# GpSimd powers in place of VectorE reciprocals for the softmax row sums of a fused attention and MLP kernel

## Chip, cores and metric

One NeuronCore of a Trainium2 chip runs the whole kernel. The metric is the device time of one execution in microseconds (us), the median of three runs.

## What is computed

Block-causal attention (8 batches, 8 heads, 576 positions, head size 64, blocks of 64), and on its output, laid out as 4608 tokens of 512 channels, a two-layer MLP with a squared ReLU:

```python
scores = scale * np.matmul(q, k.transpose(0, 1, 3, 2))
scores = np.where(block_i >= block_j, scores, -1000000000.0)
scores = scores - np.max(scores, axis=-1, keepdims=True)
attn = np.exp(scores)
attn = attn / (np.sum(attn, axis=-1, keepdims=True) + 1e-09)
x = np.matmul(attn, v)            # then transposed to tokens x channels
r = np.maximum(x @ w_in, 0.0)
out = (r * r) @ w_out
```

The change touches the division by the row sums.

## The kernel before

**Passes and groups.** Attention goes in 40 passes, each for a pair of heads of one batch: passes 0 to 7 (the first 192 positions of batches 0 and 1), 8 to 11 (the other positions of batch 0) and 12 to 39. A pass works on one to three groups of blocks of 64 query rows; the two heads fill the 128 partitions. There are 8 groups in passes 0 to 7 and three in each of the 32 others, 104 in all. A group has two, three or four blocks, so its row sums are a tile of 128 partitions by 2, 3 or 4 (`sm`).

**The steps of a group** are closures made by `rows` (line 781) and `splits`, and named by a letter and the group (`R21_2` is step R of pass 21, group 2):

- A: TensorE computes the scores into a two-bank PSUM tile (`side`).
- B: VectorE takes each row's negated maximum (`nmx`).
- C: ScalarE takes the exponential into the f32 tile `p` (two buffers; four slots of `p_rows` in passes 0 to 7) and accumulates the row sum into `sm`.
- S (`summed`, line 822): GpSimd adds 1e-9 to `sm` and scales it by a power of two.
- R (`inverse`, lines 826 to 828): VectorE takes the reciprocal of `sm` into `rs`. This is the line that changes.
- Then `p` is multiplied by `rs`. In passes 0 to 7 step D (VectorE or GpSimd) makes three diagonal matrices of `rs`, with which TensorE transposes and scales at once. In passes 8 to 11 step D (ScalarE, VectorE) writes the scaled rows. From pass 12 on, step H (ScalarE or VectorE) writes an f16 high part and step L (VectorE) the f16 rest, into `p_rows`; one step per piece of a row, `H21_2_1` being piece 1 of group `21_2`.
- From pass 12 on the rows are turned by DMA transposes issued by SP (T); then TensorE multiplies by the values (G) and the result is read out (X).

The buffer of `p` is free for a later group's C when the group's last L (or D) is done.

**The MLP** runs between these steps. TensorE multiplies in `pair` and `single` PSUM tiles; ScalarE and VectorE rescale, square and split the hidden layer into f16 parts (`r`, `hidden`), and the residual `hidden<-r,hidden` (steps `rem`) is taken by GpSimd or VectorE. In the first 120 us the weights are loaded and split into f16 parts as well: `bits` on GpSimd, `join` and `low` on VectorE, `cast` on any of the three. The normalized tokens are split by steps `t` and `s`, some on GpSimd.

**The order** is written out by hand. `ORDER` (from line 104) lists every step, with a letter where an engine has to be chosen (A ScalarE, D VectorE, P GpSimd). `Plan.run` walks through it, and the wrapper `Queue` chains each engine's instructions, so that every engine works in the order of this list, whatever is ready. A step R stands at its own place in the list, often long after its S. In 49 of the 104 groups at least one other GpSimd step stands between the two; six of them have only other S steps between. Two of the places, cut to those steps that matter here (lines 123 to 124 and 174 to 177):

```
... cast0_14:P ... R11_2 D11_1:D max1_9:A sq0_1_0 D11_2:D ...
... R21_1 po2_1_10 l232_1 H21_1_1:A S21_2 t2_15:P H21_1_2:A H21_1_0:A p64_0 a114_0 t3_9:P R21_2 L21_1_2 ...
```

Of the kernel before, what the change touches and what calls it, by code (L numbers as in the profile page):

```python
# [8 lines left out]
F32 = mybir.dt.float32  # L9
# [6 lines left out]
ALU = mybir.AluOpType  # L16
# [3 lines left out]
P = 128  # L20
# [377 lines left out]
def attention_moe_kernel(ctx: ExitStack, tc: tile.TileContext, qk1, v1, qk, ks, vm, vt, w_in, w_out, out):  # L398
    nc = Lines(tc)
    NB = vm.shape[0]  # L400

    const = ctx.enter_context(tc.tile_pool(name="const", bufs=1))
# [10 lines left out]
    def bank_of(ring):  # L413

        turns_of[ring] += 1
        return homes[ring][(turns_of[ring] - 1) % len(homes[ring])]
# [8 lines left out]
    nc.vector.memset(zero, 0.0)  # L425
    ones_bf = const.tile([P, P], BF16, name="ones_bf")
    nc.vector.memset(ones_bf, 1.0)
    vd = const.tile([P, 2], BF16, name="vd")
    nc.gpsimd.memset(vd, 0.0)

# [100 lines left out]
    def spin(region, n):  # L531


        w = region.shape[-1]
        for _ in range(n):
            nc.tensor.matmul(
                region.rearrange("p (a b) -> p a b", b=D),
                ones_bf,
                ones_bf[:, None, 0:D].to_broadcast([P, w // D, D]),
                start=True,  # L540
                stop=True,
            )
# [217 lines left out]
    def scores(t, ps, group):  # L760


        lanes = ([], [])
        for j, off in group:
            c0 = 0
            while c0 <= j:
                c1 = min(j + 1, c0 + 8 - (off // D + c0) % 8)
                o = off + D * c0
                lanes[o >= 512 if t["quad"] else 0].append((j, c0, slice(o, off + D * c1)))
                c0 = c1  # L770
        order = [(z, x) for n in range(4) for z in range(2) for x in lanes[z][n : n + 1]]
        for z, (j, c0, o) in order:
            k = slice(D * c0, D * c0 + o.stop - o.start)
            keys = t["turned"] if z else t["kf"]
            q = t["turned"][:, S:] if z and j == NJ - 1 else t["qf"][:, D * j : D * j + D]
            for r in range(2):
                rs = slice(D * r, D * r + D)
                h = 1 - r if z else r
                nc.tensor.matmul(ps[D * h : D * h + D, o], q[rs], keys[rs, k], start=True, stop=True)

    def rows(t, group):

        u = t["u"]
        n = len(group)
        gu = f"{u}_{group[0][0]}"
        box = {}
        short = t["whole"] and not t["first"]
        at = {2: 0, 1: 2 * P, 0: 3 * P} if short else dict(group)

        def score():  # L790
            ps = box["ps"] = bank_of("s")
            if t["i"] == 0:
                spin(ps[:, 512:], SPIN)
            scores(t, ps, group)

        def largest():
            ps = box["ps"]
            nmx = box["nmx"] = small.tile([P, n], F32, tag="nmx", name=f"nmx_{gu}")
            for i, (j, off) in enumerate(group):
                w = D * (j + 1)  # L800
                nc.vector.tensor_reduce(nmx[:, i : i + 1], ps[:, off : off + w], axis=AX.X, op=ALU.max, negate=True)
            nc.vector.tensor_scalar(nmx, nmx, D**-0.5, None, op0=ALU.mult)

        def raised():
            if short:
                p32 = x_rows[:, t["i"] % SLOTS].rearrange("p b k -> p (b k)")
            else:
                p32 = p2.tile([P, 1024], F32, tag="p32", name=f"p32_{gu}")
            box["p32"] = p32
            sm = box["sm"] = small.tile([P, n], F32, tag="sm", name=f"sm_{gu}")  # L810
            for i, (j, off) in enumerate(group):
                w = D * (j + 1)
                nc.scalar.activation(
                    p32[:, at[j] : at[j] + w],
                    box["ps"][:, off : off + w],
                    AF.Exp,
                    bias=box["nmx"][:, i : i + 1],
                    scale=D**-0.5,
                    accum_out=sm[:, i : i + 1],
                )  # L820

        def summed():
            sm = box["sm"]
            nc.gpsimd.tensor_scalar(sm, sm, 1e-9, 2.0**-A_P, op0=ALU.add, op1=ALU.mult)

        def inverse():
            rs = box["rs"] = small.tile([P, n], F32, tag="rs", name=f"rs_{gu}")
            nc.vector.reciprocal(rs, box["sm"])

        def spread(q="DVE"):  # L830
            if short:
                (nc.vector if q == "DVE" else nc.gpsimd).tensor_tensor(
                    x_diag[:, t["i"] % SLOTS],
                    ident[:, None, :].to_broadcast([P, n, P]),
                    box["rs"][:, :, None].to_broadcast([P, n, P]),
                    op=ALU.mult,
                )
                return
            for i, (j, off) in enumerate(group):
                w = D * (j + 1)  # L840
                o, a, rs = y_rows[:, j - 3, 0:w], box["p32"][:, off : off + w], box["rs"][:, i : i + 1]
                if q == "ACT":
                    nc.scalar.activation(o, a, AF.Copy, scale=rs)
                else:
                    (nc.vector if q == "DVE" else nc.gpsimd).tensor_scalar(o, a, rs, None, op0=ALU.mult)

        return dict(score=score, largest=largest, raised=raised, summed=summed, inverse=inverse, spread=spread), box

    def splits(group, box):
# [1167 lines left out]
```

## Time and profile before

| what | us |
|---|---|
| median of three runs (lowest, highest) | 954.14 (953.74, 954.61) |
| the profiled execution, by the same clock as the runs | 953.77 |
| its span in the profile, first to last instruction | 952.0 |
| PE (TensorE) busy | 929.8 |
| DVE (VectorE) busy | 753.0 |
| ACT (ScalarE) busy | 656.6 |
| POOL (GpSimd) busy | 238.6 |

The span is 1.8 us shorter than the profiled execution. Times in the rows are counted from the start of the span. The granted TensorE clock is 1.00 of full speed over the whole span. A busy PE can still be waiting inside a matmul whose end is modelled, and all instructions of the program carry the helper's line L331, so that rows are told apart by their tiles. The chain of waits is followed back from the last instruction: at each step to what released it, or to the instruction before it on its engine; where it stands on an engine, a shorter instruction there would have made the end earlier, until another chain takes over.

### The profile page before, as it was taken

The page shows a single profiled execution, that of the slowest core. Times are in us where ns is not written, and L with a number is a line of the kernel's source. Part 1 is how long each engine was busy: PE and PEld are TensorE (multiplying, and loading weights), DVE is VectorE, ACT ScalarE, POOL GpSimd, SP SyncE. Part 2 cuts the span into 40 slices and gives each one's busy share as a digit, 9 for nine tenths or more (in the row PEclk, how much of TensorE's full clock was granted, in tenths as well). Part 3 has the DMA queues.
Part 4 walks back from the last instruction along what each step waited for, and adds up shares of the span by engine and source line. Part 5 has one row for each costly group of instructions (what it writes and reads, how often), then busy time and mean ns, then how long its engine had stood idle before and what let it go on. Part 6 is the DMA issues. An engine that isn't in the chain of part 4 may idle for free.

```text
span 952.0 us, 21220 instructions
## 1 busy us (share of the span) xinstructions
PE 929.8 (98%) x8145; PEld 603.9 (63%) x8145; DVE 753.0 (79%) x1698; ACT 656.6 (69%) x1620; POOL 238.6 (25%) x353
## 2 busy tenths in 40 slices
PE   7799999999999999999999999999999999999998
PEld 5355554554555775686676775587666775587775
DVE  7999999899889878889898478888889567566341
ACT  7999987876886757877786547677888545343331
POOL 5654402143235311132022012121022020012210
PEclk9999999999999999999999999999999999999999
DMA  9944675876732609753863418914973405300001
GB/s 363 403 142 157 150 170 118 163 166 155 176 98 48 159 13 195 162 119 63 172 143 86 82 47 150 218 47 71 188 176 84 81 12 100 73 13 2 24 12 34
DMA packets 221651, 114.94 MB, mean 121 GB/s; under 512 B 195290, under 2 KB 203756, under 8 KB 221548
## 3 DMA queue, kind: packets, MB, share of 16 engines
q1 hardware_dynamic: 221548, 113.57, 49.7%
q8 instruction: 64, 1.05, 0.4%
q14 instruction: 39, 0.32, 0.1%
HBM read 58.21 MB, written 9.46 MB: 71 GB/s over the span
## 4 chain that ended last, share of the span: by engine, by line
PE 78%; DVE 10%; DMA 5%; ACT 5%; issue 2%; POOL 0%; SPq 0%; ACTq 0%; DVEq 0%; POOLq 0%
PE pair L331 37%; PE single L331 29%; PE side L331 12%; DVE nmx L331 2%; DVE p_rows L331 2%; DVE w L331 2%; DMA p_turned<-p_rows 2%; ACT p L331 1%; DMA turned_w<-in_w_in 1%; DMA vraw<-in_vt 1%; DMA w<-in_w_out 1%; ACT r L331 1%; ACT p_rows L331 1%; DVE xt_all L331 1%; DVE _AluOpType.subtract L331 0%
## 5 line engine op out<-in xcount | busy, mean ns | idle before, releaser
L331 PE MATMUL single<-w,hidden 128*128 128x512 f16 (+1 forms) x1488 | 335.0, 372 | 0.1
L331 PEld LDWEIGHTS <-hidden 128*128 128x128 f16 x1776 | 167.8, 98 | 174.9 <-issue 11.6
L331 PE MATMUL pair<-xt_all,w 128*128 128x192 f16 (+1 forms) x2304 | 260.2, 266 | 1.1 <-DVE xt_all L331 0.7
L331 PEld LDWEIGHTS <-w 128*128 128x128 f16 x2304 | 200.0, 98 | 55.3 <-issue 7.3
L331 ACT ACTIVATE p<-side,nmx 128x576 f32<-128x576 f32 (+8 forms) x264 | 140.0, 542 | 43.1 <-DVE nmx L331 24.2
L331 POOL TENSOR_TENSOR hidden<-r,hidden 128x384 f16<-128x384 f32 x98 | 98.7, 1017 | 225.2 <-ACT hidden L331 195.8
L331 DVE SCALAR_TENSOR_TENSOR p_rows<-p,rs,p_rows 128x128 f16<-128x128 f32 (+7 forms) x264 | 139.4, 554 | 9.4 <-ACT p_rows L331 7.8
L331 DVE TENSOR_REDUCE nmx<-side 128x1 f32<-128x64 f32 (+8 forms) x288 | 123.3, 480 | 15.0 <-PE side L331 14.5
L331 ACT ACTIVATE r<-pair,rescale 128x384 f32<-128x384 f32 x139 | 80.8, 584 | 68.5 <-PE pair L331 64.7
L331 PE MATMUL pair<-xt_all,turned_w 128*128 128x192 f16 x1296 | 124.7, 246 | 0.1
L331 ACT CAST hidden<-r 128x384 f16<-128x384 f32 x176 | 87.2, 510 | 44.7 <-DVE r L331 38.3
L331 PEld LDWEIGHTS <-turned_w 128*128 128x128 f16 x1296 | 108.9, 98 | 13.2 <-issue 2.1
L331 ACT ACTIVATE r<-r 128x384 f32<-128x384 f32 x184 | 95.3, 524 | 28.4 <-DVE r L331 25.9
L331 DVE SCALAR_TENSOR_TENSOR r<-pair,rescale,r 128x384 f32<-128x384 f32 x108 | 66.3, 614 | 57.5 <-PE pair L331 41.3
L331 POOL TENSOR_SCALAR sm<-sm 128x2 f32<-128x2 f32 (+2 forms) x104 | 32.2, 309 | 313.9 <-ACT p L331 296.9
L331 ACT ACTIVATE p_rows<-p,rs 128x64 f16<-128x64 f32 (+11 forms) x176 | 92.3, 552 | 12.2 <-DMA p_turned<-p_rows 6.8
L331 PE MATMUL side<-qk 64*64 64x512 f32 (+2 forms) x480 | 90.6, 488 | 4.2 <-ACT p L331 3.4
L331 PE MATMUL side<-ks,qk 64*64 64x192 f32 (+4 forms) x576 | 86.4, 417 | 0.0
L331 DVE TENSOR_TENSOR hidden<-r,hidden 128x384 f16<-128x384 f32 x94 | 54.2, 579 | 17.2 <-ACT hidden L331 17.0
L331 PE MATMUL pair<-w,hidden 128*128 128x512 f16 x288 | 64.6, 379 | 0.0
L331 PE MATMUL side<-p_turned,v 128*64 128x384 f16 (+3 forms) x1128 | 62.0, 265 | 1.5 <-ACT p L331 1.5
L331 PEld LDWEIGHTS <-v 128*64 128x64 f16 x1128 | 49.3, 110 | 21.8 <-issue 11.8
(153 smaller groups left out, 1008.1 us busy)
## 6 DMA issues: line engine op xcount, KB each, us to landing
qk<-in_qk SPq DMA_DIRECT2D x32, 576.0 KB
ks<-in_ks SPq DMA_DIRECT2D x32, 320.0 KB
vraw<-in_vm SPq DMA_DIRECT2D x30, 256.0 KB
w<-in_w_out SPq DMA_DIRECT2D x10, 512.0 KB
out<-ob SPq DMA_DIRECT2D x17, 256.0 KB
w<-in_w_in SPq DMA_DIRECT2D x8, 512.0 KB
out<-ob SPq DMA_DIRECT2D x26, 128.0 KB
hidden<-in_w_in SPq DMA_DIRECT2D x6, 512.0 KB
```

The costliest lines, as they stand in the source:

```text
L331: i = make(*a, **k)
```

## The change

A constant tile of -1.0 is set by GpSimd at the start, and step R becomes an elementwise power on GpSimd with that tile as exponents. The place of R in `ORDER` stays, so it stands now in GpSimd's queue, between the GpSimd steps that the list has before and after it.

```diff
@@ -425,6 +425,8 @@
     ones_bf = const.tile([P, P], BF16, name="ones_bf")
     nc.vector.memset(ones_bf, 1.0)
+    minus_ones = const.tile([P, 4], F32, name="minus_ones")
+    nc.gpsimd.memset(minus_ones, -1.0)
     vd = const.tile([P, 2], BF16, name="vd")
     nc.gpsimd.memset(vd, 0.0)
@@ -825,7 +827,7 @@
         def inverse():
             rs = box["rs"] = small.tile([P, n], F32, tag="rs", name=f"rs_{gu}")
-            nc.vector.reciprocal(rs, box["sm"])
+            nc.gpsimd.tensor_tensor(rs, box["sm"], minus_ones[:, 0:n], op=ALU.pow)
```

## Rows read from the trace of the kernel before

**Rows 1.** The page's first part: busy time, share of the span, instructions.

```profile
PE 929.8 (98%) x8145; PEld 603.9 (63%) x8145; DVE 753.0 (79%) x1698; ACT 656.6 (69%) x1620; POOL 238.6 (25%) x353
```

**Rows 2.** Stretches: length, each engine's busy time (instructions), clock, DMA share, GB/s.

```profile
31.00:41.00 10.00, 6.47 (x64) 2.90 (x64) 9.31 (x24) 9.97 (x29) 6.33 (x13) 1.00 1.04 402
41.00:91.00 50.00, 45.48 (x325) 25.59 (x327) 48.84 (x105) 48.60 (x116) 26.70 (x32) 1.00 0.49 171
91.00:121.00 30.00, 27.79 (x198) 14.62 (x194) 29.12 (x64) 29.87 (x78) 12.39 (x24) 1.00 0.68 179
121.00:277.00 156.00, 155.87 (x1195) 83.00 (x1194) 139.34 (x319) 125.38 (x313) 41.57 (x61) 1.00 0.68 150
```

**Rows 3.** The chain of waits in order of time: start, length, what it stood on.

```profile
30.82 10.04 DMA turned_w<-in_w_in
...
41.57 0.07 DVE rs L331
...
64.08 0.15 DVE rs L331
...
89.64 0.07 DVE rs L331
...
161.07 0.09 DVE rs L331
...
596.97 0.09 DVE rs L331
```

**Rows 4.** Instructions on the tile sm: ns min/median/max; then a wait for it.

```profile
L331 POOL TENSOR_SCALAR sm<-sm x104: 192/196/857, 7.7 to 808.0; 128x2 f32<-128x2 f32 x48, 128x3 f32<-128x3 f32 x32, 128x4 f32<-128x4 f32 x24
L331 DVE RECIPROCAL rs<-sm x104: 146/165/283, 7.9 to 808.2; 128x2 f32<-128x2 f32 x48, 128x3 f32<-128x3 f32 x32, 128x4 f32<-128x4 f32 x24
...
  DVE rs L331: 4.9, 7
```

**Rows 5.** The page's groups: count | busy us, mean ns of one | idle before.

```profile
L331 POOL TENSOR_TENSOR hidden<-r,hidden 128x384 f16<-128x384 f32 x98 | 98.7, 1017 | 225.2 <-ACT hidden L331 195.8
L331 POOL TENSOR_SCALAR sm<-sm 128x2 f32<-128x2 f32 (+2 forms) x104 | 32.2, 309 | 313.9 <-ACT p L331 296.9
L331 DVE TENSOR_TENSOR hidden<-r,hidden 128x384 f16<-128x384 f32 x94 | 54.2, 579 | 17.2 <-ACT hidden L331 17.0
```

**Rows 6.** Groups by line and shape, POOL: its costliest instruction by the mean.

```profile
L331 POOL TENSOR_SCALAR w<-w,wsc 128x512 f16<-128x512 f32 x9 | 14.9, 1653 | 10.4 <-DVE w L331 7.6 <-DVE m_w L331 2.6
```

**Rows 7.** Timeline around 89 us: start, length, instruction, merged count.

```profile
88.65 0.19 POOL L331 TENSOR_SCALAR sm<-sm 128x2 f32<-128x2 f32 x1
88.93 1.62 POOL L331 TENSOR_SCALAR w<-w,wsc 128x512 f16<-128x512 f32 x1
...
89.63 1.69 DVE L331 TENSOR_SCALAR p_rows<-p,rs 128x512 f32<-128x512 f32 x4
```

**Rows 8.** Timeline around 305 us; in brackets idle time before and what ended it.

```profile
304.42 0.67 ACT L331 ACTIVATE p_rows<-p,rs 128x448 f16<-128x448 f32 x1
...
305.03 1.21 POOL L331 TENSOR_TENSOR _AluOpType.subtract<-w,_AluOpType.subtract 128x512 f32<-128x512 f16 x1
...
308.25 0.53 ACT L331 ACTIVATE p<-side,nmx 128x320 f32<-128x320 f32 x1 [2.45 <-DVE p_rows L331]
...
310.08 2.16 PE L331 MATMUL side<-p_turned,v 128*64 128x192 f16 x36 [1.45 <-ACT p L331]
```

**Rows 9.** Timeline around 599 us.

```profile
599.40 0.19 POOL L331 TENSOR_SCALAR sm<-sm 128x2 f32<-128x2 f32 x1 [4.46 <-ACT p L331]
...
599.83 0.45 DVE L331 TENSOR_SCALAR p_rows<-p,rs 128x448 f16<-128x448 f32 x1
```

**Rows 10.** Timeline around 468 us, group 28_0.

```profile
467.84 0.92 POOL L331 TENSOR_TENSOR hidden<-r,hidden 128x384 f16<-128x384 f32 x1 [0.21 <-ACT hidden L331]
468.05 0.98 ACT L331 ACTIVATE p_rows<-p,rs 128x256 f16<-128x256 f32 x2
```

## The prediction

> **What bounds the kernel now.** I read the busy times first: PE is busy for 929.8 of 952.0 us [rows 1], so at most some 22 us could be won from its idle time. Then the stretches [rows 2]: the DMA engines are full until 41 us (a share of 1.04); from 41 to 91 VectorE works 48.84 of 50 us, from 91 to 121 ScalarE 29.87 of 30; from 121 on PE works nearly without a gap (155.87 of 156). The chain of waits says the same [rows 3]: a weight load that lands at 40.86, then VectorE, then ScalarE, then PE; later VectorE comes back for short pieces. What is to be seen: a reciprocal stands on this chain with far less than its own duration, 0.07 of about 0.165 us [rows 3, 4], because the next instruction starts before it has ended.
>
> **What is removed.** 104 reciprocals leave VectorE. Only their time on the chain counts. Between 41 and 91 us there are nine: eight of 0.07 and one of 0.15, together 0.71. From 161 to 597 there are nine more, of 0.07 to 0.17, together 1.00; the first and the last of both stand in [rows 3], with the one of 0.15. Gain: **1.71 us**. The two reciprocals on the chain before 41 us I cost at nothing, since the full DMA engines cover them [rows 2]; without that cover each would be worth as much as one of the others. VectorE's waits for GpSimd's scaling, 4.9 us in 7 places [rows 4], go with the reciprocal. What is late next is VectorE's own use of `rs` in the same group, so I credit nothing more for them.
>
> **What is added.** A memset at the start, for which nothing waits while the first loads are on their way; and 104 powers of 2 to 4 elements per partition on GpSimd. No row shows a power. Below, I bound it by the shortest instruction of GpSimd on the same tile, the scaling: 0.19 us [rows 4]. Above, by GpSimd's costliest instruction, 1.65 us for 512 columns [rows 6]. The nearest row is the scaling as it runs among the others, 0.31 us in the mean [rows 5]: same engine, same tile. A power has a second operand and does more than an add and a multiply, so I put one shortest instruction on top: **X = 0.5 us**, my estimate. GpSimd's time itself is no limit (238.6 of 952 us busy [rows 1]; 52 us more).
>
> The Trainium skill, GPSIMD Engine Reference, section "Key points", holds VectorE to be about twice as fast for elementwise work. The trace comes near: the same residual takes 1017 ns on GpSimd and 579 on VectorE [rows 5]. By that rule alone a power would cost about 0.33 us, and the sum below would come out near -0.9 us instead.
>
> **What is moved.** Before, `rs` was ready some 0.2 us after the scaling, when VectorE was free. Now it comes X plus a handover of about 0.05 after whatever GpSimd does ahead of it, and GpSimd works in the written order. A consumer that came late anyway sees nothing of it. SP's transposes wait for the L steps, not for GpSimd, and their order stays. Where R leaves VectorE, nothing takes its place. Three places on or beside the chain lose:
>
> 1. At 88.84 us the scaling of group 11_2 ends; ahead of R11_2 the list has R11_1 and a weight cast of 1.62 us. So `rs` is ready at 88.93 + X + 1.62 + X + 0.05 = 91.60. VectorE uses it now in the second half of the four pieces that start at 89.63 (576 of their 1472 columns, so from about 90.7) [rows 7]. Loss 2X - 0.1 = **0.90**, on the chain.
> 2. At 305 us two GpSimd subtractions stand between S21_2 and R21_2, the second ending at 306.24 [rows 8]; R21_1, ahead of S21_2, pushes them by X. `rs` comes at 306.24 + 2X + 0.05 = 307.29 instead of before 304.42, where ScalarE scales with it. From there to the next exponential ScalarE has 1.38 us of work and 2.45 us of idle time (308.25 - 304.42 in all); the idle time takes most of the delay: the exponential starts at 308.67 instead of 308.25. Loss 2X - 0.58 = **0.42**; PE waits for this exponential at 310.08.
> 3. At 599.59 nothing stands between, and VectorE wants `rs` at 599.83 [rows 9]. Loss X - 0.19 = **0.31**.
>
> Consumers before 41 us wait too, some 0.35 us each (X + 0.05 less the 0.2 of before), under the full DMA engines; if that cover were thin, I would expect up to 1 us from it. Others after 121 us lie under PE's work.
>
> **The sum.** -1.71 + 0.90 + 0.42 + 0.31 = -0.08 us against the profiled execution of 953.77, which lies 0.37 below the median of the runs. On the median: **954.1 us**, no change. With X = 0.2 it is -1.71 + 0.3 = -1.4 us, or 952.7; with X = 1.65 it is -1.71 + 3.20 + 2.72 + 1.46 = +5.7, or 959.8. A measurement of this kernel can tell about 0.2%, 1.9 us, from no change. The sum passes +1.9 us at 5X - 0.87 - 1.71 = 1.9, X = 0.9 us.
>
> **Rivals.**
>
> *The power is slow.* At X of 0.9 to 1.65 us the first consumer of `rs` becomes the wait that ends last, at the same three places and then at others. For it: a power is no primitive of the kind the rows show, and the scaling already goes up to 857 ns when others are in its way [rows 4]. Against it: the tile is tiny. 956.0 to 959.8 by the sum, to 963 where further groups join. This is the rival of the other sign, and X = 0.9 is where it decides.
>
> *The queue is slow.* Even a short power stands behind GpSimd work that waits for something else. In 49 of 104 groups another GpSimd step stands between S and R. In group 28_0 that step is a residual that waits for ScalarE and ends at 468.76; ScalarE scales with `rs` at 468.05 now, and would start at 469.31, 1.26 us late, with its evacuations of PSUM behind it [rows 10]. If ten such places cost a third of this each, 4 us: 958. Against it: the chain stands on PE there, and ScalarE has time left.
>
> *The relief is larger.* VectorE is the tightest engine from 41 to 121 us and loses instructions and waits. If the 4.9 us of waits [rows 4] are worth half, that is 2.5 us on top: 951.6. Against it: the consumer on VectorE now waits in the same place.
>
> *The first power stands long.* This would come once, near 7.9 us, while the DMA engines are full until 41 [rows 2]; GpSimd is idle for 3.7 of the last 10 us of that stretch, so a delay of some 6 us is mostly caught up: +0 to +3 us, up to 957. No row shows a first GpSimd instruction that is slow, so it has little chance. The Trainium skill, GPSIMD Engine Reference, section "Instruction dispatch", has such a cost, about 6 us at the first call of freshly loaded code; no run here shows it.
>
> That the change does nothing of what it says, I rule out: the order of every engine is written by hand and R keeps its place.
>
> **How the numbers follow.** The forecast case, X from 0.2 to 0.9 and nothing else, holds 0.46, and all of it is within 0.2%. The slow power gets 0.24, the slow queue 0.14, the first power 0.03: together 0.41 for slower. The larger relief gets 0.13, for faster. The forecast case alone spans 952.7 to 956. The range goes from 952.2, half way into the relief, to 963, the end of the slow power.
>
> **What would show it.** In the profile after: the mean duration of the power; VectorE busy some 17 us less; the chain from 41 to 91 us still on VectorE, without `rs`, and with a wait for GpSimd near 90; ScalarE or VectorE waiting for POOL `rs`, some 0.3 us at a time; PE busy as before. It is wrong if the power takes over 0.9 us, if waits for POOL `rs` add up to more than some 20 us, or if PE's idle time grows by more than 2 us after 121 us.

## The result and the profile after

The changed kernel takes 965.56 us (median of four runs, 963.80 to 965.92) against 953.94 for the kernel before beside it: a ratio of **1.0117, 95% interval 1.0099 to 1.0135**, 11.6 us slower. The forecast was 954.1 and the range ended at 963.0. The profiled execution took 965.66 us, its span 963.6.

The page's first part, as in [rows 1], and the shares of the chain of waits by engine:

```profile
PE 933.1 (97%) x8145; PEld 606.0 (63%) x8145; DVE 747.1 (78%) x1594; ACT 656.8 (68%) x1620; POOL 337.3 (35%) x458
...
PE 76%; DVE 7%; POOL 6%; ACT 5%; issue 4%; DMA 1%; ACTq 0%; POOLq 0%; DVEq 0%
```

GpSimd works 98.7 us more. VectorE is relieved of 104 instructions, but its busy time falls by only 5.9 us. The reciprocals last 17.1 us in sum, but they overlap with the instructions behind them [rows 3, 4]: in e3 below, where they are gone too, the busy time falls by 9.4 us. And here VectorE's other instructions last 3.6 us longer in sum than before. PE executes the same 8145 matmuls: of the 11.6 us by which the span grew, 8.3 are idle time of PE and 3.3 longer busy time, some of it at a lower clock. GpSimd now holds 6% of the chain.

GpSimd's groups by line and shape give the price that no row of before had (count | busy us, mean ns of one | idle before):

```profile
L331 POOL TENSOR_TENSOR rs<-sm,minus_ones 128x2 f32<-128x2 f32 x48 | 39.8, 829 | 2.8
L331 POOL TENSOR_TENSOR rs<-sm,minus_ones 128x3 f32<-128x3 f32 x32 | 30.4, 952 | 1.5
L331 POOL TENSOR_TENSOR rs<-sm,minus_ones 128x4 f32<-128x4 f32 x24 | 26.8, 1118 | 1.2
```

Together (39.8 + 30.4 + 26.8) / 104 = 0.93 us each: X was put at 0.5. That alone does not make 11.6 us: with X = 0.93 the prediction's sum is -1.71 + 1.76 + 1.28 + 0.74 = +2.1.

The stretches of [rows 2], in the same columns, with one more ahead of them:

```profile
0.00:31.00 31.00, 20.70 (x203) 15.32 (x203) 20.96 (x65) 21.92 (x76) 21.99 (x38) 1.00 0.96 368
31.00:41.00 10.00, 8.18 (x72) 5.82 (x72) 5.39 (x11) 5.83 (x15) 6.63 (x13) 0.83 1.03 400
41.00:91.00 50.00, 42.94 (x308) 23.01 (x301) 47.63 (x95) 47.09 (x114) 35.77 (x42) 0.97 0.43 149
91.00:121.00 30.00, 26.63 (x192) 14.32 (x191) 27.69 (x52) 28.46 (x74) 19.29 (x30) 1.00 0.48 146
121.00:277.00 156.00, 155.28 (x1184) 82.82 (x1183) 139.32 (x294) 127.20 (x321) 64.06 (x88) 1.00 0.62 155
```

The DMA engines are as full until 41 us as before (1.03 against 1.04), and yet VectorE and ScalarE, which worked 9.31 and 9.97 of the ten microseconds from 31 to 41 [rows 2], now work 5.39 and 5.83. And the granted clock, 1.00 before, is 0.83 there.

**Where the time went.** PE executes 8145 matmuls in both kernels in one order. I took the start of the n-th in the one trace less that of the n-th in the other, and the median of this lag over the matmuls within 0.6 us of a given time of the kernel before. For the changed kernel and, for later use, the nine experiments (one profiled execution each):

```
us of before       30    38   105   306   312   590   605   730   own time
after             6.9   6.5   8.5   8.8  11.2  11.4  10.3  11.6   965.66
e1_late_pow       0.5   0.8   2.0   2.0   4.4   4.8   3.3   4.6   958.50
e2_early_pow      7.4   6.5   6.1   5.5   5.5   5.6   4.8   4.8   958.58
e3_product        1.9   1.5   1.8   1.5   1.1   1.0  -0.2  -0.2   953.87
e4_behind         5.3   4.4   6.2   7.1   5.6   5.8   4.9   6.2   960.33
e5_spot21         0.4   0.7   2.3   2.5   2.4   2.8   1.5   2.9   956.90
e6_from12         0.6   0.7   1.6   2.2   3.2   3.9   3.0   4.4   958.18
e7_late_behind    0.6   0.8   1.4   2.6   1.1   1.3  -0.3   0.7   954.99
e8_early_dvec     3.0   3.6   3.1   2.7   2.7   2.6   1.3   1.3   955.09
e9_joined         1.3   1.3   1.2   2.8   1.3   1.4   0.7   1.8   955.64
```

So 6.5 of the 11.6 us are lost before 38 us, 2.0 more by 105, 2.4 at place 2 (306 to 312), 1.3 between 605 and 730, and 1.1 comes back around 602; the rest are small steps. The traced execution is not always near the median of its runs: that of e2 lies 1.0 us above it, that of e9 1.6 below.

**The first 38 us.** The chain of waits, from 9 to 33 us, in its shares by line and in some of its steps (start, length, what it stood on):

```profile
by line: POOL rs L331 28.1%; POOL p_rows L331 22.7%; POOL w L331 21.2%; issue 8.3%; POOL sm L331 7.9%; DVE w L331 2.9%; PE pair L331 2.9%; POOL hidden L331 2.7%; DVE stw L331 2.5%; PE single L331 1.2%; DVE st L331 0.7%; POOLq L331 0.2%
...
10.89 0.86 POOL rs L331
11.82 0.83 POOL p_rows L331
12.73 0.60 POOL sm L331
13.40 1.18 POOL rs L331
14.66 0.83 POOL p_rows L331
...
31.02 1.32 POOL p_rows L331
32.38 3.47 PE pair L331 x16
```

GpSimd's instructions hold 83% of this chain: the power (R), the diagonals that need it (D, `p_rows`), the next scaling (S), the next power, and its share of the weight work (`w`) in between. The same 24 us in both kernels show what gave way:

```profile
8.00:32.00 24.00, 20.19 (x214) 15.44 (x210) 22.44 (x63) 21.37 (x74) 16.11 (x27) 1.00 1.03 416
```

```profile
8.00:32.00 24.00, 15.51 (x172) 12.34 (x168) 19.50 (x53) 18.72 (x66) 21.83 (x30) 1.00 1.03 408
```

Before (first line) VectorE, ScalarE and PE were nearly as full as the DMA engines, so a path through them can have had little slack beside the loads. After, GpSimd is the full one, and PE does 172 matmuls in place of 214 while the DMA engines still move their share.

The waits of the changed kernel (engine, what it waited for: us in total, times, longest) have 38.6 us for `rs` on GpSimd, and three of PE for the diagonals:

```profile
DVE p_rows L331 <- POOL rs L331: 21.1, 20, 3.1
ACT p_rows L331 <- POOL rs L331: 17.5, 18, 2.3
PE pair L331 <- POOL p_rows L331: 5.9, 3, 3.5
```

**Place 1**, timeline, to be held against [rows 7]:

```profile
95.45 0.72 POOL L331 TENSOR_TENSOR rs<-sm,minus_ones 128x2 f32<-128x2 f32 x1
96.18 1.57 POOL L331 TENSOR_SCALAR w<-w,wsc 128x512 f16<-128x512 f32 x1
97.72 0.82 POOL L331 TENSOR_TENSOR rs<-sm,minus_ones 128x2 f32<-128x2 f32 x1
98.57 0.65 DVE L331 TENSOR_SCALAR p_rows<-p,rs 128x320 f32<-128x320 f32 x2 [0.61 <-POOL rs L331]
```

The order is the foretold one: power, cast, power, then VectorE's second half, late by 0.61 us.

**Place 2**, timeline, to be held against [rows 8]:

```profile
310.46 1.91 DVE L331 TENSOR_TENSOR xt_all<-x,xt_all 128x768 f16<-128x768 f32 x1
311.51 1.57 POOL L331 TENSOR_TENSOR rs<-sm,minus_ones 128x3 f32<-128x3 f32 x1
313.12 1.52 ACT L331 ACTIVATE p_rows<-p,rs 128x384 f16<-128x384 f32 x3 [2.04 <-POOL rs L331]
315.74 1.01 POOL L331 TENSOR_TENSOR rs<-sm,minus_ones 128x2 f32<-128x2 f32 x1
316.78 0.67 ACT L331 ACTIVATE p_rows<-p,rs 128x448 f16<-128x448 f32 x1 [1.68 <-POOL rs L331]
318.07 0.51 ACT L331 ACTIVATE p<-side,nmx 128x320 f32<-128x320 f32 x1
319.88 3.71 PE L331 MATMUL side<-p_turned,v 128*64 128x192 f16 x42 [2.49 <-ACT p L331]
```

ScalarE waits twice, for R21_1 and for R21_2; the idle time of 2.45 us that stood ahead of this exponential [rows 8] is gone, and PE waits 2.49 instead of 1.45 us. Then PE runs slowly; the stretches say why:

```profile
318.00:319.00 1.00, 0.00 (x0) 0.00 (x0) 0.96 (x4) 1.00 (x7) 0.00 (x0) 1.00 0.00 0
...
320.00:321.00 1.00, 1.00 (x16) 0.91 (x17) 0.64 (x1) 0.97 (x3) 0.10 (x1) 0.50 0.29 66
```

The granted clock is at 0.50, the 1.2 GHz level, after PE had stood idle; it was at 1.00 throughout before.

**Place 3 and a fourth.** Timeline:

```profile
611.41 0.45 DVE L331 TENSOR_SCALAR p_rows<-p,rs 128x448 f16<-128x448 f32 x1 [1.15 <-POOL rs L331]
...
719.83 1.22 POOL L331 TENSOR_TENSOR rs<-sm,minus_ones 128x4 f32<-128x4 f32 x1
721.09 0.35 ACT L331 ACTIVATE p_rows<-p,rs 128x64 f16<-128x64 f32 x1 [1.34 <-POOL rs L331]
...
724.28 1.15 PE L331 MATMUL pair<-xt_all,w 128*128 128x192 f16 x12 [0.70 <-DVE r L331]
```

At place 3 VectorE waits 1.15 us, but PE loses nothing there: its lag falls by 1.1 us at 602 (a wait of PE for ScalarE of 0.65 us that the kernel before had at 601.65 is no longer there, which explains the larger part of it). Near 720 a power makes ScalarE and VectorE late, and PE with them: from 605 to 730 the lag grows by 1.0 to 1.4 us in every run with powers in the late passes, and not at all in e2, e3 and e8. This place was not in the prediction.

### The profile page after: what moved, and what is told of

Its sections match the earlier page's. It is cut to its first block, busy times and chain, and to the rows that moved or that the text cites. A ratio compares the mean times of both kernels' runs of the same rounds, so it can differ in the third digit from the quotient of the medians.

```text
span 963.6 us, 21219 instructions
## 1 busy us (share of the span) xinstructions
PE 933.1 (97%) x8145; PEld 606.0 (63%) x8145; DVE 747.1 (78%) x1594; ACT 656.8 (68%) x1620; POOL 337.3 (35%) x458
## 4 chain that ended last, share of the span: by engine, by line
PE 76%; DVE 7%; POOL 6%; ACT 5%; issue 4%; DMA 1%; ACTq 0%; POOLq 0%; DVEq 0%
PE pair L331 36%; PE single L331 28%; PE side L331 12%; POOL rs L331 2%; DVE nmx L331 2%; ACT p L331 2%; DVE p_rows L331 1%; ACT r L331 1%; DVE w L331 1%; POOL p_rows L331 1%; POOL w L331 1%; POOL _AluOpType.subtract L331 1%; ACT p_rows L331 1%; POOL hidden L331 1%; DVE xt_all L331 1%
## 5 line engine op out<-in xcount | busy, mean ns | idle before, releaser
L331 PEld LDWEIGHTS <-hidden 128*128 128x128 f16 x1776 | 167.7, 98 | 175.0 <-issue 11.6
L331 POOL TENSOR_SCALAR sm<-sm 128x2 f32<-128x2 f32 (+2 forms) x104 | 35.9, 345 | 262.7 <-ACT p L331 248.5
L331 ACT ACTIVATE p_rows<-p,rs 128x64 f16<-128x64 f32 (+11 forms) x176 | 91.9, 551 | 21.6 <-POOL rs L331 17.5
L331 POOL TENSOR_TENSOR rs<-sm,minus_ones 128x2 f32<-128x2 f32 (+2 forms) x104 | 97.0, 934 | 5.5
```

Of the source, the lines that this page charges most:

```text
L331: i = make(*a, **k)
```

## The experiments

Four questions: early passes or late ones (e1, e2), the move or the length of the power (e3), where the power stands in GpSimd's queue (e4, e7, e9, and e8 for the diagonals behind it), and single places (e5, e6). All start from the changed kernel; the edits of e5 and e6 are shown against e1. e1 to e4 stood beside runs of the kernel before with a median of 953.76 us, e5 to e8 beside 954.08, e9 beside 954.65; a difference between experiments of two such batches holds this shift, and is given against the kernel before as well. Single executions spread: the twelve of e7 go from 954.99 to 959.96 us, nine of them below 956, the five of e9 from 955.64 to 959.66.

**e1: VectorE's reciprocal back in passes 0 to 7.**

```diff
-            nc.gpsimd.tensor_tensor(rs, box["sm"], minus_ones[:, 0:n], op=ALU.pow)
+            if short:
+                nc.vector.reciprocal(rs, box["sm"])
+            else:
+                nc.gpsimd.tensor_tensor(rs, box["sm"], minus_ones[:, 0:n], op=ALU.pow)
```

> Passes 0 to 7 take VectorE's reciprocals as before, the 96 later groups the power. Theory A (GpSimd's queue has become the chain between 10 and 32 us and sets 6.6 of the 11.6 us): 959.0 us (958 to 960), PE's first matmul of pass 8 on as early as before. Rival B (the loss comes from later consumers that wait for rs, and the early delay is caught up under the loads): 963 us or more.

958.97 us, ratio 1.0053 (1.0038 to 1.0068). Eight of the 104 powers carry 6.6 us of the 11.6 (6.4 against the kernel before beside each). The lag at 38 us is 0.8 instead of 6.5; from there to 730 us it grows by 3.8 us, against 5.1 in the changed kernel.

**e2: the reverse, powers in passes 0 to 7 only.** The two branches are exchanged.

> The power in passes 0 to 7 alone (8 groups), VectorE's reciprocals in the 96 others. Theory A: 960.5 us (959.5 to 961.5), all of the loss made before 45 us. Rival B: 954 to 956.

957.63 us, 1.0038 (1.0025 to 1.0051): 3.9 us, between the two expectations. The early loss is all there (lag 7.4 at 30 us, 6.5 at 38), but with reciprocals behind it 1.7 us come back on the way to the end: 1.0 between 38 and 306 us, and 0.7 later, around 602, where the changed kernel gets time back as well. The two halves alone cost 5.2 + 3.9 = 9.1 us, together 11.6. That part of what each costs alone hides in idle time that the other also needs would fit the lags, but was not tested by itself, and which idle time between 38 and 306 us gives it back was not singled out.

**e3: a product in the power's place.** Everything stays where the change put it; only the operation is a short one. `rs` is then -sm, so the rows are scaled by minus their sum and not by its reciprocal.

```diff
-            nc.gpsimd.tensor_tensor(rs, box["sm"], minus_ones[:, 0:n], op=ALU.pow)
+            nc.gpsimd.tensor_tensor(rs, box["sm"], minus_ones[:, 0:n], op=ALU.mult)
```

> Every step R stays on GpSimd at its place in the order, but multiplies the sums by -1 instead of taking the power, so rs is not the reciprocal. Length theory (the 0.93 us of a power make the loss): the product takes 0.2 to 0.35 us and the whole 953 to 956 us. Place rival (it is the place behind other GpSimd steps, in a queue that waits): 960 us or more, with DVE and ACT still waiting for POOL rs over 20 us in total.

953.15 us, 0.9993 (0.9984 to 1.0003). GpSimd's groups by shape, and the waits:

```profile
L331 POOL TENSOR_TENSOR rs<-sm,minus_ones 128x2 f32<-128x2 f32 x48 | 15.7, 329 | 2.8
L331 POOL TENSOR_TENSOR rs<-sm,minus_ones 128x3 f32<-128x3 f32 x32 | 8.7, 272 | 1.5
L331 POOL TENSOR_TENSOR rs<-sm,minus_ones 128x4 f32<-128x4 f32 x24 | 7.2, 299 | 1.2
```

```profile
DVE p_rows L331 <- POOL rs L331: 8.5, 12, 1.6
ACT p_rows L331 <- POOL rs L331: 5.9, 6, 1.4
```

At 0.30 us in the mean (31.6 / 104) the same move costs nothing, and the waits for `rs` fall from 38.6 to 14.4 us. The length of the power is the cause, not the engine, the handover or the place by itself. What the relief of VectorE is worth alone, e3 does not show: the 0.6 us that it wins by the medians (1.5 faster to 0.3 slower by the interval) still holds the waits for the products.

**e4: each power right behind its scaling.** R follows S in `ORDER` at once.

```diff
+_R = [w for w in ORDER.split() if not (w[0] == "R" and w[1].isdigit())]
+ORDER = " ".join(x for w in _R for x in ((w, "R" + w[1:]) if w[0] == "S" and w[1].isdigit() else (w,)))
```

> The power everywhere, but each R moved in the written order to stand right behind its S. Length theory: the early part is unchanged (the sum of GpSimd's work counts there, not its order) and the whole stays at 964 to 967 us, since GpSimd's other steps now wait for the powers. Place rival: the 49 groups that stood behind another step get rs earlier, and 3 to 5 us come back: 960.5 to 962.5.

960.36 us, 1.0067 (1.0050 to 1.0084): 5.2 us come back with powers as long as before (0.95 us in the mean), a little more than the place rival had. VectorE's waits for `rs` fall from 21.1 to 12.4 us, ScalarE's from 17.5 to 6.1. The lag is 4.4 at 38 us, so the early loss is mostly still there. At place 2 it is 5.8 us at 300, 7.1 at 306 and 5.6 at 312: nothing is lost across the place, where the changed kernel loses 2.4. ScalarE waits 0.30 us for `rs` there instead of 1.68, and PE goes on without a wait (the helper's line is L333 in this kernel):

```profile
311.56 0.67 ACT L333 ACTIVATE p_rows<-p,rs 128x448 f16<-128x448 f32 x1 [0.30 <-POOL rs L333]
...
315.67 2.26 PE L333 MATMUL side<-p_turned,v 128*64 128x192 f16 x42
```

**e5: e1, and the reciprocal also in the groups 21_1 and 21_2** (place 2).

```diff
-            if short:
+            if short or (t["i"] == 21 and group[0][0] != 4):
```

> As e1, and the two groups 21_1 and 21_2 take VectorE's reciprocals too. If the loss near 310 us comes from their powers in GpSimd's queue, the step of 2.7 us that PE falls behind there goes, and the whole is 956.3 us (955.5 to 957.2). If it is only where an earlier delay comes to light, it stays at 958.5 or more.

956.89 us, 1.0027 (1.0016 to 1.0039), 2.1 less than e1 (2.4 against the kernel before beside each). Timelines of e1 and of e5 at place 2, and the stretch from 300 to 325 us in both:

```profile
309.98 0.67 ACT L331 ACTIVATE p_rows<-p,rs 128x448 f16<-128x448 f32 x1 [1.67 <-POOL rs L331]
...
313.07 3.89 PE L331 MATMUL side<-p_turned,v 128*64 128x192 f16 x42 [2.49 <-ACT p L331]
...
300.00:325.00 25.00, 22.51 (x196) 15.13 (x194) 19.54 (x36) 17.08 (x44) 17.28 (x18) 0.93 0.43 98
```

```profile
310.61 0.53 ACT L331 ACTIVATE p<-side,nmx 128x320 f32<-128x320 f32 x1 [2.45 <-DVE p_rows L331]
...
312.43 2.26 PE L331 MATMUL side<-p_turned,v 128*64 128x192 f16 x42 [1.30 <-ACT p L331]
...
300.00:325.00 25.00, 23.59 (x215) 15.62 (x214) 23.26 (x43) 17.76 (x47) 16.31 (x16) 1.00 0.49 114
```

With reciprocals ScalarE has its 2.45 us of idle time back, PE's wait falls from 2.49 to 1.30 us, and the clock stays at 1.00: the 42 matmuls take 2.26 instead of 3.89 us. Place 2 is worth 2.1 to 2.4 us: 1.2 of the wait, and the rest came with the clock.

**e6: reciprocals in passes 0 to 11, powers from 12 on** (so place 1 is out).

```diff
-            if short:
+            if t["whole"]:
```

> As e1, and passes 8 to 11 take VectorE's reciprocals too (powers from pass 12 on). If place 1 of the prediction (group 11_2 behind 11_1 and a cast) and its neighbours cost what PE falls behind before 50 us in e1, 1.0 to 1.6 us come back: 957.4 us (956.8 to 958.2). Rival (these groups are hidden): 959.0, no change to e1.

957.67 us, 1.0036 (1.0024 to 1.0048). The time is the expected one, but the trace does not put it at place 1, which stands near 91 us [rows 7] and not before 50, as the expectation had it. At 91 us the lag is 1.0 below that of e1, at 105, behind place 1, only 0.4, and the larger difference comes at place 2. There ScalarE waits for `rs` as in e1, and PE as long:

```profile
313.32 2.26 PE L331 MATMUL side<-p_turned,v 128*64 128x192 f16 x42 [2.51 <-ACT p L331]
```

but the clock stayed at 1.00 in this execution. So the same wait, 2.49 and 2.51 us, was followed by 3.89 us of work in one and 2.26 in the other, and the lag grew there by 2.4 us in e1 and by 1.0 in e6. What place 1 costs is not settled by e6.

**e7: e1, with the powers from pass 8 on right behind their scaling** (e4's edit for the groups with "_" in their names).

> As e1, with each of the 96 powers moved right behind its S. Place theory for the late part (powers come late for standing behind GpSimd's other steps): most of the 5.2 us goes, 954.5 to 956. Length theory alone: 958 to 960.

955.57 us, 1.0026 (1.0014 to 1.0037), 3.4 less than e1 (3.7 against the kernel before beside each). VectorE's waits for `rs` fall from 19.4 to 10.4 us, ScalarE's from 16.1 to 5.8. The later loss was mostly one of place in the queue.

**e8: e2, with the diagonals D1 to D7 on VectorE instead of GpSimd.**

```diff
-D1:P ... D2:P ... D7:P
+D1:D ... D2:D ... D7:D
```

> As e2 (powers in passes 0 to 7 alone), with the seven diagonal steps D of these passes that GpSimd had given to VectorE. If GpSimd's filled queue is what costs 3.9 us there (8 powers of 0.9 and 7 diagonals of 0.83 us in it), 5.8 us of GpSimd's work leave and 3 to 4 us come back: 953.8 to 955. If it is the length of the chain S, R, D alone, about 957 stays (the diagonal gets only 0.3 us shorter each).

955.09 us, 1.0006 (0.9998 to 1.0015), 2.5 less than e2 (2.9 against the kernel before beside each) and just past the end of the expected 953.8 to 955. The stretch to 41 us, in e2 and in e8:

```profile
0.00:41.00 41.00, 29.98 (x269) 22.38 (x273) 25.73 (x74) 27.13 (x90) 27.43 (x50) 0.92 0.98 376
```

```profile
0.00:41.00 41.00, 29.08 (x281) 20.34 (x283) 32.17 (x89) 29.98 (x98) 23.49 (x45) 1.00 0.97 375
```

GpSimd works 3.9 us less, VectorE and ScalarE 6.4 and 2.9 more in the same time, the clock is at 1.00 again, and PE has no wait for GpSimd's diagonals left (5.1 us in e2). The eight powers are as long as in e2 (0.93 and 0.96 us in the mean). The lag at 38 us falls from 6.5 to 3.6, and later to 1.3. So nearly half of what was lost by 38 us, and most of what stayed of it, came from the diagonals in GpSimd's queue, which had D behind R behind S.

**e9: e4 and D1 to D7 on VectorE together**, all 104 powers kept.

> The power in all 104 groups, each right behind its S (as e4), and the seven diagonal steps on VectorE (as e8). If the two causes are the whole of it, the early loss falls to about 1 us and the late one to about 1.5: 956.5 us (955.3 to 957.5). If the power's length costs as much as before wherever it stands, 959 or more.

957.23 us, 1.0039 (1.0025 to 1.0052). The lag at 38 us is 1.3: the two moves take 5.2 of the 6.5 us, about the sum of what each takes alone (2.1 in e4, 2.9 in e8). What is left in the end is 2.6 us by the medians and 3.7 by the ratio, so the two causes account for 8 to 9 of the 11.6 us; 1.1 of the rest stands at the place near 720 (lag 0.7 at 605, 1.8 at 730). It is still slower than the kernel before, and no version tried here that computes the reciprocal beats that one.

## Why the prediction was wrong

- **The step that failed: "Consumers before 41 us wait too, some 0.35 us each ... under the full DMA engines; if that cover were thin, I would expect up to 1 us from it."** They cost 6.5 us by 38 us (lag), 6.6 by e1, 3.9 alone (e2). I read the chain of waits, which names the DMA engines up to 40.86 [rows 3], as if all else there had slack. It shows only the path that ended last. VectorE at 22.44, ScalarE at 21.37 and PE at 20.19 of 24 us were the sign that a second path had little slack. And the 0.35 us was reckoned per consumer, where eight groups pass one after the other through one queue: a power and the diagonals that need it hold GpSimd and make the next scaling late, so the delays add up.
- **X = 0.5 us was mis-sized**: 0.93 in the mean, 0.69 at the least. The mean lay within the bounds (0.19 to 1.65), though single powers took up to 2.12 us, and 0.93 lies just past the 0.9 from which the prediction itself had "slower". The estimate added a second operand to the scaling; e3 shows that the operand is nearly free (0.30) and the operation is what costs. The Trainium skill, GPSIMD Engine Reference, section "Key points", holds VectorE about twice as fast for elementwise work; here the power takes 0.93 us against 0.165 for the reciprocal [rows 4], 5.7 times as long, so its rule does not carry over to this operation.
- **The gain of 1.71 us** is neither shown nor refuted: e3, with the reciprocals gone and a short instruction in their place, is 0.6 us faster by the medians (0.3 slower to 1.5 faster). At the product's 0.30 us the sum gives 5 x 0.30 - 2.58 = -1.1, which the interval holds. VectorE's busy time was to fall by some 17 us and fell by 5.9, since the reciprocals had overlapped with other instructions; the gain itself had been counted by the 0.07 on the chain.
- **Place 1, 2X - 0.1:** mechanism right, row by row. With the 0.72 and 0.82 us of the two powers there it would be 1.4; VectorE's wait is 0.61, and the lag grows by 1.1 us from 62 to 105 in the changed kernel and by nothing in e1, which has the same two powers there; in e6, which has none, it grows by 0.4. Its cost stays open between 0 and 1.1.
- **Place 2, 2X - 0.58:** 1.28 at X = 0.93, measured 2.4 by the lag and 2.1 by e5. Two things were missing: R21_1 makes ScalarE wait as well, since it took 1.57 us beside a VectorE instruction with two inputs, and PE's clock fell to the 1.2 GHz level after the wait.
- **Place 3, X - 0.19:** the wait is there (1.15 us), the loss is not. A place near 720 us, which I did not list, costs 1.2 instead.
- **The path behind it:** the chain from 41 to 91 us was to stay on VectorE; PE holds 42% of it now. PE's idle time after 121 us grows by 2.1 us (5.8 to 7.9), just past the 2 us that were named as a sign of being wrong, and PE is busy for 3.3 us more, where it was to be as before.
- **The rivals.** "The power is slow" gave the sign, and its end, 963, came within 2.6 us of the time; but at X = 0.93 it had about 956.2, for want of the early passes, so that this nearness is luck. "The queue is slow" was right in kind: with the same powers, e4 wins 5.2 us and e7 3.4 by place alone. They were not alternatives but one mechanism, a long instruction in a queue that others are waiting behind. "The first power stands long" fell: the first, at 7.81 us, took 0.87, like the others. The sign that I had named, over 20 us of waits for POOL `rs`, came at 38.6.

## What to carry to other kernels

When the chain of waits stands on one resource, look at how busy the other engines are in the same stretch before costing anything there at nothing: the chain shows one path, and the next may end only a moment earlier. An operation without a row is better bounded by a test of that operation than by its neighbours on the same tile, and its price can be paid again by each instruction that waits behind it in the queue. After a move to an in-order queue, put the moved step right behind its input and look at who stands behind it.

## What the runs showed of the hardware

**A power on GpSimd** takes 829, 952 and 1118 ns in the mean for 2, 3 and 4 columns. Those of them beside which VectorE executes no instruction with two inputs in SBUF take 0.73, 0.87 and 1.02 us (24, 15 and 11 powers), so about 145 ns per column on some 440; the others take 0.93, 1.02 and 1.20. A product of the same tiles takes 0.30 us whatever their width.

**Beside VectorE it runs longer.** Timeline of the longest power of the changed kernel:

```profile
115.17 1.76 DVE L331 TENSOR_TENSOR x<-x,hb 128x1536 f32<-128x1536 f32 x1
115.37 2.12 POOL L331 TENSOR_TENSOR rs<-sm,minus_ones 128x2 f32<-128x2 f32 x1
```

It ends 0.56 us after VectorE's instruction with two inputs has ended (117.49 and 116.93); at place 2 it is 0.71 us (313.08 and 312.37). The Trainium skill, SBUF — State Buffer, section "Who interferes with whom", says that a VectorE instruction with two inputs in SBUF contends with a GpSimd instruction that reads SBUF; these rows and the means above agree. No run changed it by itself.

**The clock** fell after PE had waited 2.49 us (e1) and did not after 2.51 us (e6); at the lower level the same 42 matmuls took 3.89 instead of 2.26 us. What decides between them, no run here shows.
